# The rows between FFN forward and backward, stored by chunk of tokens instead of by feature group, with the order of the steps made anew

## The chip, the cores and the metric

The kernel runs on one core of a Trainium2 chip. The time is device microseconds of one execution, and the figure compared is the median of several. A core has a matrix engine (PE, whose weight loads the profile lists apart as PEld), three engines for elementwise work (VectorE or DVE, ScalarE or ACT, GpSimd or POOL), and SyncE (SP), which here only issues DMA transfers. Each engine works through its own list of instructions in order. A transfer is issued from the list of SP, ACT or POOL and lands some microseconds later; those of one list are issued one behind the other, and an issue that has to wait holds up all behind it.

## The reference

A block with a residual, and all of its gradients, in bf16:

```python
x = A_u                                   # 2048 tokens x 512 features
xn = layernorm(x)
s = conv_S4(xn, A, B, C, dt) + xn * Dskip # per feature a convolution of 2048 taps
g = silu(silu(xn @ w1) @ w2)              # w1 512x1792, w2 1792x512
out = x + s * g
# outputs: out, and the gradients for A_u, A_re, A_im, B_re, B_im,
#          C_re, C_im, log_dt, Dskip, w1, w2, from grad_out
```

The taps are `K = Re(sum over n of C P dB)` with `P = exp(dt A l)`, n of 128 states. The reference does the convolution by an FFT, the kernel by matrix products with DFT tables.

## The kernel before

The kernel is written as some forty generators, each a stream of steps: one step issues one block of matmuls, one eviction of PSUM, one elementwise instruction or one transfer. `PLAN` is seven strings, and every letter of them runs the next step of one stream; the order in the string is so the order on every engine. `SLOTS` gives the buffer that each tile takes. `WAYS` says for each stream which engine does its n-th PSUM eviction: A is ACT (line 116), D is DVE (line 117). Streams that the text speaks of:

- `F` (`gen_ffn_fwd`): for each of 8 chunks of 256 tokens, h = xn w1 in 7 pairs of feature groups (ps_h, L769), evicted to the tile `hT`, silu on ACT (L777), the product with w2 (ps_o, L786). The rows h, before silu, are stored to `Hd` in DRAM from POOL's list (`k.st`, L779), 8 feature groups and then 6.
- `X`, `C`: the forward convolution (ps_s L406, pt_f L420, ps_i L451 and L464, with evictions to `dA`, `dB`, `KE`). `R`: the taps (ps_k, L657, evicted to `ds`). `Kb` is a piece of the taps, read back.
- `D`, `B`: the same transforms for the gradient. `a`: loads h back from `Hd` into `dhT` (L1142, SP), `A`: multiplies with the gradient that comes through w2 (ps_da, L1174; L1177 on DVE) and stores the product to `DHd`. `x`: its product with w1 (ps_dx, L1198), evicted to `pd_s` or, for the last four, added on DVE (L1203).
- `Y`, `V`, `T`, `S`, `Z`: the gradients of the taps' parameters. In 32 halves of blocks `V` makes `Vb` (ps_v, L1026, evicted to `Vb`), `T` three products on DVE (L1043 twice, L1047), `S` a sum on PE (psS, L1063), `Z` the rest (L1087 to L1133).
- `h`, `t`, `w`: dW2. For each of 14 feature groups h is loaded back from `Hd` as `h_in` (L1217, SP), turned on PE and passed through silu (`a_tok`, L1228), and multiplied (ps_w, L1237), with an eviction to `o`. `g`, `v`: dW1, from `DHd`, by transposing loads `dh_tok` (L1252, SP) and ps_w (L1266) with evictions to `o` of 128x256.
- `i`, `k`, `m`: LayerNorm backward (L1307 on).

`Hd` is a tile of [14, 128, 2048]: feature group, feature, token. A store of a chunk therefore writes, for each feature and group, a run of 256 tokens or 512 bytes. The load of `dhT` reads the same runs. The load of `h_in` reads one feature group with all tokens, in runs of 4096 bytes. `DHd` lies in the same way.

Of the kernel before, what the change touches and what calls it, by code (L numbers as in the profile page):

```python
# [13 lines left out]
BF16 = mybir.dt.bfloat16  # L14
# [4 lines left out]
P = 128  # L19
# [27 lines left out]


SLOTS = dict(x.split("=") for x in """
fp.XT=01010101;pf.pf=012010210210210210201201201201210201201201201201201021021021012012012010210210210120120120120120210  # L50
210210210212010120120120120201202102102102102102102102102102102012012012102102102102101021012021021201021021012012120120
2102102012021021021021021;fp.hT=0101010101010101;fp.ob=0101010;dft.w8=21031230123102302103213032013201;pc.pc=01010101010
100010101010101010101010101010101010101010101010101010101101010101010101010101010101010101010101010101010101010101010101
010101010101010101010101010101010101001011010101010101010101010101010101011010101010101010101110101010101010010101010101
010101010101010;tbl.tv=01011010001010100101001011101010;tbl.ts=01010101010111011101010111010010;tbl.W=010101101011010110
10;dft.t4=010100101010;gate.S=01;gate.g=10672345;da.doT=01010101;da.dhT8=20120120;dftb.w8b=1010;da.dhT6=10101010;go.go_s
=01010101;go.go_r=010101;go.go_g=01010101;go.go_x=01201201;da.pd_s=010101010101;sb.YT=0120120120120120;sb.Eb=10101010;sb
.Gb=01010101;sb.Vb=0101010101010101;sb.Tp=0101010101010101;sb.Sa=1010;fw.h_in=01201201201201;fw.a_tok=10101010101010;fw.
o11=01201201201201;sb.g_acc=0101;fw.dh_tok=0120120;fw.o10=1010101;lw.pd_l=012301;lw.Gt=01230123;lw.m=010101;lw.o1=123012
30  # L60
""".replace("\n", "").split(";") if x)

WAYS = """J=DADAADAA;
F=DADAAAAAAAADDADAAAAAAAADAAAAAAAAAAAAAAAAAAADADDAAAAAAAAADAADDAADADDADAAA;
# [5 lines left out]
D=AAAADDAAAAAAAAADAAAAADAAAADAADAAAADAAADA;  # L72
d=DDAADDAA;
B=AAAAAAAAAADAAADAAAAAAAAAAAAAAAAAAAAAAAAAAAAADAAAAAAADAAD;
x=AAAAAAADAADD;
V=DAADAAAAADAAAAAADDAAAAAAAAAAAAAAAAAAAAAAAAAAAAAAAAAAAAAAAAAAAAAA;
Y=AAADDAAA;
w=ADAADAAAAAAAAA;
v=DAAAAAAAAAAAADAAAAAAAAAAAAAA"""


class Placed:
# [672 lines left out]
def gen_ffn_fwd(k):  # L755
    nc, fp = k.nc, k.fp
    D, FT, DK, T = k.D, k.FT, k.DK, k.T
    for c in range(T // 2):
        cs = slice(256 * c, 256 * c + 256)
        XTv = k.XT.pop(c)[:].rearrange("p (t k) n -> p t k n", k=DK)  # L760
        aT = fp.tile([P, FT, 256], BF16, name="aT", tag="aT", bufs=1)
        for f in range(FT // 2):
            if f in (0, 4):
                hT = fp.tile([P, 8, 256], BF16, name="hT", tag="hT", bufs=2)
            ps = k.pf.tile([P, 2, 256], F32, name="ps_h", tag="pf")
            for j in range(2):
                ft = 2 * f + j
                for dk in range(DK):
                    nc.tensor.matmul(out=ps[:, j], lhsT=k.W1[:, dk, ft * P:ft * P + P], rhs=XTv[:, :, dk, :],  # L769
                                     start=(dk == 0), stop=(dk == DK - 1))  # L770
            yield
            i = 2 * (f % 4)
            k.ev(hT[:, i:i + 2, :], ps[:])
            yield
            if f in (3, 6):
                f0, n = (0, 8) if f == 3 else (8, 6)
                nc.scalar.activation(out=aT[:, f0:f0 + n], in_=hT[:, 0:n], func=ACT.Silu)  # L777
# [558 lines left out]
def kernel(ctx, tc, A_u, A_A_re, A_A_im, A_B_re, A_B_im, A_C_re, A_C_im, A_log_dt, A_Dskip, B_x, B_w1, B_w2, grad_out,  # L1336
           out_0, out_1, out_2, out_3, out_4, out_5, out_6, out_7, out_8, out_9, out_10, out_11):
    nc = tc.nc
    k = KCtx()
    k.nc, k.tc = nc, tc  # L1340
    k.outs = [out_0, out_1, out_2, out_3, out_4, out_5, out_6, out_7, out_8, out_9, out_10, out_11]
    L, D, F = A_u.shape[1], A_u.shape[2], B_w1.shape[1]
    assert (L, D, F) == (2048, 512, 1792)
    k.L, k.D, k.F, k.T, k.DK, k.FT = L, D, F, 16, D // P, F // P
# [94 lines left out]
    sb = pool("sb", side="right", es=es_b)  # L1439
# [5 lines left out]
    fw = pool("fw")  # L1445
# [5 lines left out]
    lw = pool("lw", side="right")  # L1451
# [30 lines left out]
```

## Time and profile before

| | |
|---|---|
| runs | 575.15, 575.63, 578.03 us, median 575.63 |
| profiled execution | 573.44 us, span 571.7 |
| PE busy | 526.4 us (92%), weight loads 395.3 (69%) |
| DVE busy | 520.0 us (91%) |
| ACT busy | 446.6 us (78%) |
| POOL busy | 75.7 us (13%) |
| DMA moved | 144.49 MB, mean 253 GB/s |

The span is the part of the execution from the first to the last instruction in the profile. The busy times overlap, so that no sum of them is a time: an engine's share says how much room its list has, and the waits say which of the lists is late. Of a wait for several things the profile names the last to come, and where the named engine had long been done, a transfer is the likely one.

### The profile page before, as it was taken

The page shows a single profiled execution, that of the slowest core. Times are in us where ns is not written, and L with a number is a line of the kernel's source. Part 1 is how long each engine was busy: PE and PEld are TensorE (multiplying, and loading weights), DVE is VectorE, ACT ScalarE, POOL GpSimd, SP SyncE. Part 2 cuts the span into 40 slices and gives each one's busy share as a digit, 9 for nine tenths or more (in the row PEclk, how much of TensorE's full clock was granted, in tenths as well). Part 3 has the DMA queues.
Part 4 walks back from the last instruction along what each step waited for, and adds up shares of the span by engine and source line. Part 5 has one row for each costly group of instructions (what it writes and reads, how often), then busy time and mean ns, then how long its engine had stood idle before and what let it go on. Part 6 is the DMA issues. An engine that isn't in the chain of part 4 may idle for free.

```text
span 571.7 us, 14504 instructions
## 1 busy us (share of the span) xinstructions
PE 526.4 (92%) x5983; PEld 395.3 (69%) x6008; DVE 520.0 (91%) x817; ACT 446.6 (78%) x561; POOL 75.7 (13%) x164
## 2 busy tenths in 40 slices
PE   2499997999989989999999999999899999999994
PEld 1365876687768765876686766787578797786763
DVE  8999998999899959999999798979889999983994
ACT  6989998999989749998998776754476876754552
POOL 4251101010101020000000000000000030332122
PEclk9879999999999999999999999999999999999998
DMA  9988998998998988787978998898999989999693
GB/s 238 321 313 221 291 227 245 341 211 264 326 230 243 345 275 314 240 265 210 345 227 265 284 286 279 241 236 180 282 215 243 208 238 222 231 237 241 171 240 120
DMA packets 156643, 144.49 MB, mean 253 GB/s; under 512 B 83488, under 2 KB 132896, under 8 KB 153504
## 3 DMA queue, kind: packets, MB, share of 16 engines
q1 hardware_dynamic: 146816, 120.74, 79.2%
q0 software_dynamic: 6640, 19.67, 10.1%
q10 hardware_dynamic: 3120, 3.15, 1.7%
q8 instruction: 47, 0.77, 0.5%
q14 instruction: 20, 0.16, 0.1%
HBM read 62.78 MB, written 59.25 MB: 213 GB/s over the span
## 4 chain that ended last, share of the span: by engine, by line
PE 48%; DVE 17%; ACT 14%; issue 9%; DMA 8%; SPq 2%; POOL 1%; POOLq 0%; ACTq 0%; DVEq 0%
PE ps_dx L1198 7%; PE ps_da L1174 7%; PE ps_w L1237 5%; PE ps_w L1266 4%; PE ps_o L786 3%; PE ps_i L451 3%; PE ps_h L769 3%; ACT dA L116 3%; PE ps_i L464 3%; ACT mag_all L518 3%; PE pt_t L138 2%; PE ps_s L406 2%; DMA Ed<-ds 2%; ACT dB L116 2%; DMA dh_tok<-DHd 2%
## 5 line engine op out<-in xcount | busy, mean ns | idle before, releaser
L116 ACT CAST dA<-ps_s 128x1024 bf16<-128x1024 f32 x82 | 82.2, 1035 | 7.3 <-PE ps_s L406 5.1
L769 PE MATMUL ps_h<-XT,W 128*128 128x256 bf16 x448 | 59.5, 286 | 9.3 <-ACT hT L116 8.4
L116 ACT CAST Vb<-ps_v 128x672 bf16<-128x672 f32 x59 | 42.2, 733 | 27.7 <-PE ps_v L1026 17.9
L769 PEld LDWEIGHTS <-W 128*128 128x128 bf16 x448 | 44.4, 102 | 18.0 <-issue 9.8
L1174 PE MATMUL ps_da<-doT,W 128*128 128x256 bf16 x448 | 56.2, 273 | 0.0
L1266 PE MATMUL ps_w<-dh_tok,xn 128*128 128x256 bf16 x448 | 52.5, 273 | 0.7 <-DMA dh_tok<-DHd 0.4
L786 PE MATMUL ps_o<-W,aT 128*128 128x512 bf16 x213 | 50.3, 385 | 2.2 <-ACT aT L777 1.4
L1198 PE MATMUL ps_dx<-W,dhT 128*128 128x512 bf16 x224 | 50.9, 379 | 0.0
L1237 PE MATMUL ps_w<-YD,a_tok 128*128 128x512 bf16 x210 | 49.1, 379 | 1.3 <-ACT o L116 0.7
L116 ACT CAST dB<-ps_i 128x1024 bf16<-128x1024 f32 x42 | 41.6, 1029 | 8.1 <-PE ps_i L451 8.0
L1266 PEld LDWEIGHTS <-xn 128*128 128x128 bf16 x448 | 43.0, 98 | 6.6 <-issue 1.0
L1174 PEld LDWEIGHTS <-W 128*128 128x128 bf16 x448 | 41.6, 98 | 7.1 <-issue 0.8
L1177 DVE TENSOR_TENSOR dhT<-ps_da,dhT 128x512 bf16<-128x512 f32 x56 | 37.8, 686 | 5.5 <-PE ps_da L1174 3.9
L786 PEld LDWEIGHTS <-aT 128*128 128x128 bf16 x224 | 21.4, 99 | 27.0 <-issue 2.5
L1198 PEld LDWEIGHTS <-dhT 128*128 128x128 bf16 x224 | 21.1, 98 | 24.8 <-issue 1.6
L1237 PEld LDWEIGHTS <-a_tok 128*128 128x128 bf16 x224 | 21.6, 98 | 24.1 <-issue 0.8
L1228 ACT ACTIVATE a_tok<-pt_t 128x1024 bf16<-128x1024 bf16 x28 | 28.7, 1038 | 7.0 <-PE pt_t L138 6.9
L406 PEld LDWEIGHTS <-TF 128*128 128x128 bf16 x384 | 25.3, 101 | 8.3 <-issue 6.0
L584 ACT ACTIVATE sn<-V 128x1920 bf16<-128x1920 int16 x16 | 29.3, 1840 | 1.8 <-DVE V L580 1.7
L477 DVE TENSOR_TENSOR cm<-sp_in,dA 128x2048 bf16<-128x2048 bf16 x24 | 29.3, 1221 | 0.6
L479 DVE TENSOR_TENSOR sp_in<-sp_in,dA 128x2048 bf16<-128x2048 bf16 x24 | 29.3, 1222 | 0.6
L451 PE MATMUL ps_i<-I,sp_in 64*128 64x128 bf16 x768 | 27.2, 217 | 2.6 <-ACT KE L116 1.4
(243 smaller groups left out, 1230.6 us busy)
## 6 DMA issues: line engine op xcount, KB each, us to landing
Yd<-YD SPq DMA_DIRECT2D x8, 1024.0 KB, 5.6
sp_in<-Ud SPq DMA_DIRECT2D x8, 1024.0 KB, 8.3
h_in<-Hd SPq DMA_DIRECT2D x14, 512.0 KB, 5.6
Ed<-ds SPq DMA_DIRECT2D x8, 672.0 KB, 7.4
Eb<-Ed SPq DMA_DIRECT2D x8, 672.0 KB, 5.7
Hd<-hT POOLq DMA_DIRECT2D x8, 512.0 KB, 6.7
Ud<-dA SPq DMA_DIRECT2D x8, 512.0 KB, 7.3
KXd<-dA SPq DMA_DIRECT2D x4, 1024.0 KB, 6.4
```

Source lines behind the costliest of these rows:

```text
L116: return self.nc.scalar.copy(out=out, in_=in_)
L406: nc.tensor.matmul(out=ps[:, j], lhsT=k.TF[:, 8 * h + j, c, :], rhs=U(8 * h + j), start=True, stop=True)
L451: nc.tensor.matmul(out=ps[:, z, g], lhsT=Y[zs, c, g0 + g, :], rhs=k.I2[zs, c].rearrange("p c m -> p (c m)"), start=(c == 0), stop=(c == 1))
L477: TT(out=t2[:], in0=b[:, :, gs], in1=a[:, 1:2, gs].to_broadcast([P, 2, n, P]), op=ALU.mult)
L479: TT(out=b[:, :, gs], in0=b[:, :, gs], in1=a[:, 0:1, gs].to_broadcast([P, 2, n, P]), op=ALU.mult)
L769: nc.tensor.matmul(out=ps[:, j], lhsT=k.W1[:, dk, ft * P:ft * P + P], rhs=XTv[:, :, dk, :], start=(dk == 0), stop=(dk == DK - 1))
L786: nc.tensor.matmul(out=ps[:], lhsT=aT[:, ft, t * P:t * P + P], rhs=k.W2[:, ft, :], start=(ft == 0), stop=(ft == FT - 1))
L1174: nc.tensor.matmul(out=ps[:, j], lhsT=k.W2[:, ft, dk * P:dk * P + P], rhs=dTv[:, :, dk, :], start=(dk == 0), stop=(dk == DK - 1))
L1177: nc.vector.tensor_tensor(out=dh[:, i0:i0 + 2, :], in0=ps[:], in1=dh[:, i0:i0 + 2, :], op=ALU.mult)
L1198: nc.tensor.matmul(out=ps[:], lhsT=dhs[ft // 8][:, ft % 8, t * P:t * P + P], rhs=k.W1[:, :, ft * P:ft * P + P], start=(ft == 0), stop=(ft ...
L1237: nc.tensor.matmul(out=ps[:], lhsT=at[:, t, :], rhs=k.do[:, t, :], start=(t == 0), stop=(t == k.T - 1))
L1266: nc.tensor.matmul(out=ps[:], lhsT=k.xn[:, t, dk * P:dk * P + P], rhs=dh[:, t].rearrange("p j n -> p (j n)"), start=(t == 0), stop=(t == k ...
```

## The change

`Hd` becomes a tile of [8, 128, 14, 256]: chunk, feature, feature group, token in the chunk. The store writes a run of 4096 bytes for each feature (8 groups) or of 3072 (6 groups), and the load of `dhT` reads these. The load of `h_in` reads for each feature eight runs of 512 bytes, one of each chunk. What arrives in SBUF is the same. `DHd` is as it was.

```diff
@@ gen_ffn_fwd
-                k.st(k.Hd[f0:f0 + n, :, cs].rearrange("f p n -> p f n"), hT[:, 0:n])
+                k.st(k.Hd[c][:, f0:f0 + n, :], hT[:, 0:n])
@@ gen_da_loads
-            k.nc.sync.dma_start(dh[:, 0:n], k.Hd[f0:f0 + n, :, 256 * c:256 * c + 256].rearrange("f p n -> p f n"))
+            k.nc.sync.dma_start(dh[:, 0:n], k.Hd[c][:, f0:f0 + n, :])
@@ gen_dw2_loads
-        k.nc.sync.dma_start(h[:].rearrange("p t n -> p (t n)"), k.Hd[ft])
+        k.nc.sync.dma_start(h[:].rearrange("p (c u) n -> p c (u n)", u=2), k.Hd[:, :, ft, :].rearrange("c p n -> p c n"))
@@ pools
-    k.Hd = dr.tile([k.FT, P, L], BF16, name="Hd")
+    k.Hd = dr.tile([8, P, k.FT, 256], BF16, name="Hd")
@@ PLAN (the first line of the first string)
-22123515255p676p41674560J777577673J77077776757p71737607775p71777F87776FF3F6F7F867706168F644F760F663666786F487373636667F3F
+2311223p55556672641376p706176J3776747717pJ3576750F6776776761F637F78778707F706675p736636776770F7F65F7446466F86773F7663678
...
@@ WAYS
-F=DADAAAAAAAADDADAAAAAAAADAAAAAAAAAAAAAAAAAAAADADDAAAAAAAAADADAADDAADADDADAAA;
+F=DADAAAAAADADADAAAAAAAAADAAAAAAADAAAAAAAAAAAAADDAAAAAAAAADADDADADDADADDADAAA;
-R=DAAAAAAAAAAAAAAAAAADAADDDADADAAAAAAAADAAAAAAAAAA;
-C=DDDAAAAAAAAAAAAAAAAADDAAAAAAAADAAAAAADADDAADADAAADDDDDADAAAAAAAA;
+R=DAAAAAAAAAAADDAAAAADAAADDDDADAAAAAAAADDAAADDAAAA;
+C=DADAAAAAAAAAAAAAAAAADDAAAAADAAADAAAAAAADAAAAADDAADADAADDDDDADAAAAAAAA;
-D=AAAADDAAAAAAAAADAAAAADAAAAADAADAAADAAADAADA;
-d=DDAADDAA;
-B=AAAAAAAAAADAAADAAAAAAAAAAAAAAAAAAAAAAAAAAAAAADAAAAAAAADAAD;
-x=AAAAAAADAADD;
-V=DAADAAAAADAAAAAADDAAAAAAAAAAAAAAAAAAAAAAAAAAAAAAAAAAAAAAAAAAAAAAA;
-Y=AAADDAAA;
+D=AAAADDAAAAAAAAADAAADAAAAAAAADAAAAAAAAAAA;
+d=DDAAADAD;
+B=AAAAAAAAAADAAADAAAAAAAAAADADAAAAAADAAAADDAAAAAAAAAAAADADA;
+x=ADADDADDADAA;
+V=ADDAAADAAADAAAAADAAAAAADAADAAADAAAADAADADDAADADAAAAAAAAAAAAAAAAA;
+Y=DAAAAAAA;
-v=DAAAAAAAAAAAAADAAAAAAAAAAAAA
+v=AADDDADAADADAADAAAAAAAAAAAAAA
```

The tables are new throughout, and no step is added or left out. Evictions on DVE go from 90 to 110, those on ACT down by as many. Three places show what the tables do.

ACT in the head of the program, one piece of the difference. `mag_all` are magnitudes of the powers, `hT` the first rows of the FFN.

```order
 L513 ACT_TABLE_LOAD
 L513 ACTIVATE dt<-ldt 128x512
-L518 ACTIVATE mag_all<-lamr 128x8x64 x27
-L116 CAST hT<-ps_h 128x512
-L518 ACTIVATE mag_all<-lamr 128x8x64 x3
+L518 ACTIVATE mag_all<-lamr 128x8x64 x21
+L116 CAST hT<-ps_h 128x512
+L518 ACTIVATE mag_all<-lamr 128x8x64 x9
 L287 ACT_TABLE_LOAD
 L287 ACTIVATE warm<-onesf 128x1
```

The first eviction of `hT` moves forward by six steps of `mag_all`; the sum of these ahead of the table load stays 30.

DVE behind the last L1203, among the products of `T`, before:

```order
L1047 TENSOR_TENSOR Tp<-Tp,Tq 128x21x64
L117 CAST o_7164<-ps_w_7165 128x256
L1043 TENSOR_TENSOR Tp<-Vb,Eb 128x16x21x4
L117 COPY YT<-pt_y 128x1024
L1043 TENSOR_TENSOR Tq<-Vb,Eb 128x16x21x4
L1047 TENSOR_TENSOR Tp<-Tp,Tq 128x21x64
L1043 TENSOR_TENSOR Tp<-Vb,Eb 128x16x21x4
L1043 TENSOR_TENSOR Tq<-Vb,Eb 128x16x21x4
```

and the corresponding place now:

```order
L117 CAST Vb<-ps_v 128x672
L1043 TENSOR_TENSOR Tp<-Vb,Eb 128x16x21x4
L1043 TENSOR_TENSOR Tq<-Vb,Eb 128x16x21x4
L117 CAST o_7243<-ps_w_7358 128x256
L1047 TENSOR_TENSOR Tp<-Tp,Tq 128x21x64
L1043 TENSOR_TENSOR Tp<-Vb,Eb 128x16x21x4
L1043 TENSOR_TENSOR Tq<-Vb,Eb 128x16x21x4
L1047 TENSOR_TENSOR Tp<-Tp,Tq 128x21x64
L1043 TENSOR_TENSOR Tp<-Vb,Eb 128x16x21x4
L117 CAST Vb<-ps_v 128x672
```

Evictions of `Vb` and `o` that ACT did stand among DVE's products now, and the copy of `YT` has gone to ACT. In all DVE has behind the last L1203 9 evictions of `Vb` (2 before), 7 of `o` of 128x256 (2 before) and no `YT` (2 before); the rest of its list there is the same.

SP at the first loads of `dh_tok`, before (`Yn` and `Eb` belong to `Y`):

```order
L1217 DMA h_in<-Hd 128x2048
L1005 DMA Eb<-Ed 128x2688
L987 DMA Yn<-Yd 128x1024
L1252 DMA_TRANSPOSE dh_tok<-DHd 128x16x128 x2
L987 DMA Yn<-Yd 128x1024
L1217 DMA h_in<-Hd 128x2048
L1000 DMA_TRANSPOSE YT<-Yd 128x8x128 x2
L1217 DMA h_in<-Hd 128x2048
```

and now:

```order
L1005 DMA Eb<-Ed 128x2688
L1217 DMA h_in<-Hd 128x8x256
L987 DMA Yn<-Yd 128x1024
L1252 DMA_TRANSPOSE dh_tok<-DHd 128x16x128
L1217 DMA h_in<-Hd 128x8x256
L987 DMA Yn<-Yd 128x1024
L1252 DMA_TRANSPOSE dh_tok<-DHd 128x16x128
L1000 DMA_TRANSPOSE YT<-Yd 128x8x128 x2
```

The two halves of a `dh_tok` pair, which followed each other, have one load of `h_in` between them.

More of the change, by code (lines that the diff above doesn't have):

```diff
@@ new lines @@
+78FF8FF8F776F7F6F485F78/XJJFPFXFFXFXPXXFFXQXFFFPPFPJFFFFPFPFFJFFPFFUX9FQFPFQXXFRXXUFXRQFFXFQQQPQXJQFPQQFQPXRFPRXFRRRXFRF
+XFFPFQFFRQQQXXRFFQXUXFQFRRFRQFQQXJXPRFQRFPUXRPRPRRFFFRQRFFRRPFXQJRRJQXPPRRRXRRQFRXFRQFQCRFQXQFFQFRQXPQFXFFPRXRXRXFPCPRRR
+CQCPRXCRCCCFCQRUFFQRCRQCQQCCFCXFPQFXRQCQFCFCCFQPCQQCFRCRPXFRPRXRRFXFRRCCFQCQFXXCQCXRQFRPFCFQCFCCRRFRCFPRQXRCJRFQFFQCXRFR
+QRQFCCFCRPPCRXRCRPXJPPRRCCXFXFXQRFXCXPQFXFCXQXFQQQPFQCRFCXFFCFCQCRRCFUCQCQRPRFFFFQRFCCCFFCFRCFCFRCRJQCCRCCRRPRCPCXQCXFCC
+RQXXXCJPXRCQPQQQFFCQRCXPCRRRXQFCQCCFRRRCFRQCCFFXXRRFCFRCPRXPQRXFXXPFFRCCFRRFURFXCFFQXRCXFQRCCFCQCJCFQQRFCCCRRFQQQRFCQCCR
@@ new lines @@
+CRCRRRRCCFRRCCCRCRRCRRQRURCRCRCRCCC/JFCGCFCCGFGCFCGGCCCFFFFGCFCGCCGGFCCFCCFGCCGFGFCCCFFGCFGFCHCCFCGGFGGGGWCCHGCFGHFMCCFG
+CCCCCFCWGFCCCCHCCCWCGWWCWCCCWHDDGWWHWWHHCCCCWWLWDDWGWDWDWDDLWWWWMWWCDDDDLMWLLWDMWDMDDDD/addDDDdAEsWDasDdBDAAAoBoAABaAAoE
+ADABDADBABaBADDBAAADBABDosDABBAAAlBDABABOEDABBaoABADDBBOsoDxBBDBoBBBBAxxBBdABBOAlBoBOBOoxsOoDaOxDBAlxBBOBBBdoDADBBExoODx
+aDBDoxBOxDBsBBAlOAoBBBABoABxoDOdDBBBBdBBABAODBaADBoAADBAADBABAEBBBBsAAdAADDBBAAABOOABaDDoAoBOABBABODOOADlDoBsAxOxDAdoDox
+sDOABDAEoBDBBAOxxDAlAxDBBOoOABBxAOBDAABoaADBoBOAOBDABDdBAOABBODBxBBBoBDaDBDDxADxoBBxOBsxDBAOAAExOADBOoBsBABBoDAAdxBBDBBB
@@ L53 @@
[L53 to L57, printed above, removed]
@@ L58 @@
-.Gb=01010101;sb.Vb=0101010101010101;sb.Tp=0101010101010101;sb.Sa=1010;fw.h_in=01201201201201;fw.a_tok=10101010101010;fw.
-o11=01201201201201;sb.g_acc=0101;fw.dh_tok=0120120;fw.o10=1010101;lw.pd_l=012301;lw.Gt=01230123;lw.m=010101;lw.o1=123012
-30
+fp.XT=01010101;pf.pf=012012012012010212102102121221201201201201201201202102102102102102102101201201201021021021021021201
+201201201202121021201021021212102120120101010120120120120201201201201021021021021021021021020102102012120121010210210210
+1021012012012012121201210;fp.hT=0101010101010101;dft.w8=21031230123103103210320103120132;pc.pc=0101011010101101010101010
@@ new lines @@
+100101010101010101010010101010101010101010101010101010101010101010101101010101010101010101010101010101010110101010101010
+101011010101010101010101010101010101010101010101010101010101101010110101010101010010101010010111010101010101010100101010
+1;fp.ob=0101010;tbl.tv=01010110001010100101110101010101;tbl.ts=01011101010111010010101011010010;tbl.W=010101101011010110
+10;dft.t4=010100101010;gate.S=01;gate.g=10672345;da.doT=01010101;da.dhT8=01201201;dftb.w8b=1010;da.dhT6=10101010;go.go_s
+=01010101;go.go_r=010101;go.go_g=01010101;go.go_x=01201201;da.pd_s=101010101010;sb.YT=2012012012012012;sb.Eb=01010101;sb
@@ L61 @@
+.Gb=01010101;sb.Vb=0101010101010101;sb.Tp=0101010101010101;sb.Sa=0101;fw.h_in=01201201201201;fw.a_tok=10101010101010;fw.
+o11=01201201201201;sb.g_acc=0101;fw.dh_tok=0120120;fw.o10=1010101;lw.pd_l=012301;lw.Gt=10231023;lw.m=010101;lw.o1=120312
+03
 """.replace("\n", "").split(";") if x)
 WAYS = """J=DADAADAA;
-F=DADAAAAAAAADDADAAAAAAAADAAAAAAAAAAAAAAAAAAADADDAAAAAAAAADAADDAADADDADAAA;
+F=DADAAAAAADADADAAAAAAAAADAAAAAAADAAAAAAAAAAAAADDAAAAAAAAADADDADADADDADAAA;
 X=AAAAAAAAAAAAAAAAAAAAAAAAAAAAAADA;
@@ L78 @@
+d=DDAAADAD;
+B=AAAAAAAAAADAAADAAAAAAAAADADAAAAAADAAAADDAAAAAAAAAAAADADA;
+x=ADADDADDADAA;
+V=ADDAAADAAADAAAAADAAAAAADAAADAAAADAAADAADDAADADAAAAAAAAAAAAAAAAAA;
+Y=DAAAAAAA;
 w=ADAADAAAAAAAAA;
-v=DAAAAAAAAAAAADAAAAAAAAAAAAAA"""
+v=AADDDADAADADADAAAAAAAAAAAAAA"""
 class Placed:
```

32 lines of the change are left out of this document (8 added, 24 removed).

## The prediction

> **What bounds the kernel now.** I read the windows first, cut where the work changes: head to 40 us, forward convolution with the first FFN matmuls to 200, the rest of that to 245, the backward convolution with the FFN's gradients to 408.4, the kernel's gradients with dW2 and dW1 to 510.2, the end of these to 528.5, LayerNorm backward behind.
>
> ```profile
> 0.00:40.00 40.00, 20.39 (x120) 13.47 (x122) 37.22 (x102) 33.42 (x51) 17.48 (x67) 0.87 0.99 289
> 40.00:200.00 160.00, 151.63 (x1910) 115.06 (x1917) 155.15 (x203) 151.56 (x180) 15.58 (x21) 1.00 0.90 268
> 200.00:245.00 45.00, 41.28 (x547) 31.73 (x548) 36.73 (x46) 35.63 (x40) 4.93 (x8) 0.96 0.83 278
> 245.00:408.40 163.40, 161.85 (x1894) 117.95 (x1891) 150.15 (x203) 123.67 (x130) 6.48 (x12) 1.00 0.89 255
> 408.40:510.20 101.80, 99.42 (x1094) 78.65 (x1101) 98.17 (x157) 73.90 (x117) 17.00 (x31) 1.00 1.07 231
> 510.20:528.50 18.30, 18.20 (x168) 13.37 (x168) 7.76 (x24) 7.75 (x13) 5.53 (x10) 1.00 1.11 249
> 528.50:564.00 35.50, 33.58 (x267) 25.10 (x268) 34.81 (x88) 20.64 (x36) 8.20 (x14) 1.00 0.79 206
> ```
>
> The columns are the window, its length, then busy us of PE, PE's weight loads, DVE, ACT and POOL, the granted clock, the DMA share and GB/s. To 245 PE, DVE and ACT are all loaded and no one engine bounds. From 245 to 408.4 PE does (161.85 of 163.4), and DVE has 13.2 us free. In the fifth window PE has 2.4 us free, DVE 3.6, ACT 27.9: DVE and PE run in lockstep there. In the last, DVE has 0.7 us free. Which of the two sets the pace of the fifth, the groups on DVE in it show:
>
> ```profile
> L1047 DVE TENSOR_TENSOR Tp<-Tp,Tq 128x1344 bf16<-128x1344 bf16 x27 | 23.1, 855 | 0.6
> L1043 DVE TENSOR_TENSOR Tp<-Vb,Eb 128x1344 bf16<-128x1344 bf16 x27 | 23.0, 853 | 2.5 <-ACT Vb L116 2.4
> L1043 DVE TENSOR_TENSOR Tq<-Vb,Eb 128x1344 bf16<-128x1344 bf16 x27 | 23.0, 852 | 0.0
> L117 DVE CAST Vb<-ps_v 128x672 bf16<-128x672 f32 x2 | 1.7, 854 | 0.0
> L117 DVE COPY YT<-pt_y 128x1024 bf16<-128x1024 bf16 x2 | 1.4, 688 | 0.3 <-PE pt_y L991 0.3
> L117 DVE CAST o<-ps_w 128x256 bf16<-128x256 f32 x1 | 0.4, 418 | 0.0
> ```
>
> Three products for each of 27 blocks fill DVE, and of its 3.6 us of idle time 2.4 are waits for a Vb that ACT evicts. The chain through these products runs from the last addition of ps_dx (L1203), which lets DVE go on to them alone, to psS on PE and the last gradients. Beginning and end, with two rows that give the step from start to start of one Vb and one o:
>
> ```profile
> 407.70 0.69 DVE L1203 SCALAR_TENSOR_TENSOR ds<-ps_dx,ds 128x512 bf16<-128x512 f32 x1 [0.66 <-PE ps_dx L1198]
> ...
> 414.02 0.85 DVE L117 CAST Vb<-ps_v 128x672 bf16<-128x672 f32 x1
> 414.78 0.85 DVE L1047 TENSOR_TENSOR Tp<-Tp,Tq 128x1344 bf16<-128x1344 bf16 x1
> ...
> 520.91 0.42 DVE L117 CAST o<-ps_w 128x256 bf16<-128x256 f32 x1 [1.96 <-PE ps_w L1266]
> 521.25 0.27 DVE L1131 TENSOR_TENSOR g_acc<-pd,dt 1x128 bf16<-1x128 f32 x1
> 528.53 0.69 DVE L1307 SCALAR_TENSOR_TENSOR pd_l<-pd_l,ds 128x512 bf16<-128x512 bf16 x1 [7.01 <-ACT a_tok L1228]
> ```
>
> **The change, part by part: DVE behind the last L1203.** Up to there PE's list has the same length, and behind it DVE's lists differ only in evictions: Vb 2 before and 9 now, o of 128x256 2 and 7, YT 2 and 0. A Vb costs 414.78 - 414.02 = 0.76, an o 521.25 - 520.91 = 0.34, a YT its 0.69 less the overlap of 0.09 that Vb shows (0.85 against 0.76), 0.60. So DVE gets 7 x 0.76 + 5 x 0.34 - 2 x 0.60 = 5.32 + 1.70 - 1.20 = +5.8 us. ACT is relieved of as many, but its 27.9 free us show that it was not the bound. At most the work fills all of DVE's 3.6 us of idle time and 2.2 us show; at least nothing of it and 5.8 do. I take half of the 2.4 us of Vb waits as saved (a Vb made on DVE itself is no longer waited for from ACT, but some 43 of 52 stay there), 1.2, so **+4.6**. What is late next is Tp, hence psS, and the lists on PE behind it.
>
> In one sentence beside this, a rule that speaks for the upper end: the Trainium skill, page "Perfetto Trace Analysis", section "Identifying the Most-Contended Engine", calls matmul busy time a poor measure for the tensor engine, takes weight-load busy time instead, and names the engine of highest occupancy as the one to look at. By it the fifth window is DVE's (98.17 of 101.8, 96%, against 78.65, 77%, for weight loads), all 5.8 us would show, and the median come out at 581.4 instead of 580.2; the row of 2.4 us of waits for ACT is why I don't take all.
>
> **DVE and ACT ahead of it.** Of all evictions DVE does 90 before and 110 now: the ten net ones above, and ten ahead of the last L1203. There dA goes from 14 to 9, ds of ps_k from 6 to 12, dB of ps_i from 6 to 9 and pd_s from 3 to 6; of seven other kinds five have one more and two one less.
>
> ```profile
> L117 DVE CAST dA<-ps_s 128x1024 bf16<-128x1024 f32 x14 | 16.8, 1220 | 6.5 <-PE ps_s L406 6.0 <-PE ps_s L434 0.5
> L117 DVE CAST dB<-ps_i 128x1024 bf16<-128x1024 f32 x6 | 7.3, 1222 | 0.6 <-PE ps_i L451 0.4
> L117 DVE CAST ds<-ps_k 128x336 bf16<-128x336 f32 x6 | 3.0, 498 | 0.0
> L117 DVE CAST pd_s<-ps_dx 128x512 bf16<-128x512 f32 x3 | 2.1, 684 | 0.0
> ```
>
> 6 x 0.50 + 3 x 1.22 + 3 x 0.68 - 5 x 1.22 = 3.0 + 3.7 + 2.0 - 6.1 = +2.6 us, and the net three others at most 3 x 1.22 = 3.7 more. The dB and pd_s, and most of the rest, fall in the PE-bound window to 408.4, whose 13.2 free us on DVE cover even 6.3; if that cover were gone it would cost between 2.6 and 6.3. Term 0.
>
> **Waits in the convolution.** The steps are mixed anew. The single waits on PE that a new mix can reach are these:
>
> ```profile
> 94.23 1.05 PE L406 MATMUL ps_s<-Kb,TF 128*128 128x128 bf16 x16 [2.17 <-DMA Kb<-KE]
> 168.57 0.62 PE L451 MATMUL ps_i<-I,sp_in 64*128 64x128 bf16 x16 [1.39 <-ACT KE L116]
> 212.09 1.86 PE L406 MATMUL ps_s<-Kb,TF 128*128 128x128 bf16 x16 [2.30 <-issue]
> 213.75 1.86 PE L769 MATMUL ps_h<-XT,W 128*128 128x256 bf16 x8
> ```
>
> Ahead of the first, eight more ps_h matmuls now stand between ps_f and Kb, 1.9 us by the row of such a block at 213.75, so it may go from 2.17 to 0.3; the place of 212.09 is the same as before. Against it stands what three more ps_k on DVE delay there, 3 x 0.50 = 1.5. Term 0, from -1.9 to +1.5.
>
> **Head.** ACT does 30 magnitude steps, now 21 ahead of the first hT and 9 behind, where it was 27 and 3. The sum is the same, so the second hT and the silu behind it stay where they are.
>
> ```profile
> PE pt_t L138 <- DVE xn L390: 10.0, 1, 10.0
> PE ps_h L769 <- ACT hT L116: 8.4, 2, 4.3
> 28.65 1.91 ACT L777 ACTIVATE aT<-hT 128x2048 bf16<-128x2048 bf16 x1
> ```
>
> The loads of x stand earlier on SP, so the first wait of 10.0 us may shrink, but what is won waits again for that silu at 28.65. Term 0; at most +1 if the W1 parts, now behind x, come late.
>
> **The store, the two loads and the queues.** Rows of DMA issues (KB each, median us to landing) and one of the queues:
>
> ```profile
> q0 software_dynamic: 6640, 19.67, 10.1%
> h_in<-Hd SPq DMA_DIRECT2D x14, 512.0 KB, 5.6
> Hd<-hT POOLq DMA_DIRECT2D x8, 512.0 KB, 6.7
> dhT<-Hd SPq DMA_DIRECT2D x8, 512.0 KB, 6.5
> dh_tok<-DHd SPq DMA_TRANSPOSE x14, 7.2
> 483.31 11.22 DMA dh_tok<-DHd
> PE ps_w L1266 <- DMA dh_tok<-DHd: 0.4, 1, 0.4
> ```
>
> The store goes over POOL's queue, q0, whose packets are 19.67 MB / 6640 = 3.0 KB already though the runs are 512 B; no engine's waits name it. Term 0. The dhT load gets longer runs, by the nearest row (h_in, 4 KB runs, the same bytes) 5.6 for 6.5 us; it runs ahead of its use and saves nothing. The h_in load gets 512 B runs, by the dhT row 6.5 for 5.6, 0.9 each, 14 times. Three h_in buffers cover the tile itself. But the DMA share in the fifth window is 1.07, and the transposes of dh_tok, queued behind h_in on SP, arrive just as PE wants them: 11.2 us on the chain, PE late by 0.4, once. Two h_in ahead of one pair: +1.8; the other way, the 0.4 goes: -0.4. I take 0, since 6.5 us are still less than the 7.2 of a transpose and the pairs now stand with one h_in between their halves.
>
> The Trainium skill, page "DMA: Bandwidth & Descriptors", section "Specifications", puts the least transfer for line rate at 512 B. By it the h_in load in runs of just that length loses nothing and the sum is the same; by the dhT row it lands 0.9 us later each time. Where the two differ, the row decides, and rival 3 stands on it.
>
> **Tail.** POOL's gout and g_acc stores now stand without an out store ahead of them, which frees half a microsecond at best; DVE's first L1307 at 528.53 had waited 7.01 us, put down to an a_tok long done, so for stores that land. The list of DVE from L1307 is the same. Term 0, from -0.5.
>
> **Sum.** The profiled execution took 573.44 us, its span 571.7, so 1.7 lie around it; the median of the runs, 575.63, stands 2.2 above it. 573.4 + 4.6 = 578.0 for an execution like the profiled one, and **580.2** as a median. From 575.63 half a per cent, 2.9 us, is about what a measurement tells from no change: 572.75 to 578.5.
>
> **Rivals.** (1) Faster: the new mix takes the three waits of 2.17, 2.30 and 1.39 (5.9) from the convolution and the last L1203 comes that much earlier, while DVE swallows the evictions down to 2.2. Then 573.4 + 2.2 - 5.9 + 2.2 = 571.9. It decides once L1203 is 5.1 earlier with 2.2, or 7.5 with 4.6. For it: one place grew by eight matmuls. Against: the place of 212.09 is the same, and up to 200 us three engines are over 94% busy. (2) Same: DVE's 3.6 us of idle time absorb all they can, since more Vb there mean fewer waits for ACT: 573.4 + 2.2 + 2.2 = 577.8. It holds if the Vb waits are gone. (3) Slower by the loads: h_in in 512 B runs makes each of seven dh_tok pairs late by 0.9, and PE, with 2.4 free, waits each time: 4.6 + 6.3 less the 0.4 that PE waits now, 573.4 + 10.5 + 2.2 = 586.1. For it the DMA share of 1.07; against it PE waited for dh_tok once in all. (4) The longer runs of the store and dhT do nothing at all: that is in the forecast, as both terms are 0.
>
> **How the numbers follow.** The forecast 0.50 (its own range 578.6 to 582.5), rival 1 0.13, rival 2 0.27, rival 3 0.10. Faster 0.13, same 0.27, slower 0.50 + 0.10 = 0.60. The range goes from 574.0, rival 1's waits with 4.6 in the fifth window (574.3), to 586.0, rival 3.
>
> **What would show it.** Of after: L1203's last row within 2 us of 407.7; DVE's Vb row in the stretch behind it with 9 and the wait of Tp for Vb on ACT below 2.4; that stretch to the last Tp longer by some 4.6 than 101.8; the h_in row near 6.5 and dhT near 5.6; PE's wait for dh_tok below 1.8. If L1203 moves by more than 3 us either way, the new mix of the convolution, not the evictions, made the time, and the prediction is wrong even if its number is near.

## The result: 1.4% slower, and the profile after

The changed kernel takes 583.94 us as a median (581.91 to 584.63), the kernel before 575.39. The ratio is 1.0138, with a 95% interval of 1.0093 to 1.0183. The profiled execution of the changed kernel took 584.63 us at a span of 582.8. So the two profiles stand 11.2 us apart where the medians stand 8.5: the profiled execution of before was the shortest of its runs, that of after the longest.

The span can be cut at five events that both kernels have: the first ps_da on PE, the last row of L1203 on DVE (its accumulator read), the start of the last L1047, the first L1307, and the end of the span. Windows of before with these cuts (window, its length, busy us of PE, PEld, DVE, ACT, POOL, granted clock, DMA share, GB/s):

```profile
0.00:248.90 248.90, 216.72 (x2614) 162.59 (x2626) 233.01 (x357) 224.50 (x272) 37.99 (x96) 0.97 0.89 271
248.90:408.30 159.40, 158.33 (x1851) 115.52 (x1849) 146.15 (x193) 119.68 (x126) 6.48 (x12) 1.00 0.90 258
408.30:509.40 101.10, 98.72 (x1089) 78.03 (x1096) 97.47 (x158) 73.42 (x117) 17.00 (x31) 1.00 1.07 231
509.40:528.50 19.10, 19.00 (x175) 14.09 (x175) 8.56 (x24) 8.32 (x14) 5.53 (x10) 1.00 1.11 248
528.50:571.70 43.20, 33.58 (x267) 25.10 (x268) 34.82 (x88) 20.64 (x36) 8.74 (x15) 0.95 0.68 179
```

The same of after:

```profile
0.00:246.70 246.70, 216.10 (x2604) 160.58 (x2617) 234.24 (x361) 223.41 (x267) 35.40 (x96) 0.98 0.87 274
246.70:409.60 162.90, 159.62 (x1855) 115.91 (x1853) 150.13 (x199) 118.15 (x121) 6.48 (x12) 1.00 0.85 254
409.60:518.70 109.10, 100.50 (x1094) 78.67 (x1104) 102.80 (x167) 68.48 (x106) 16.53 (x30) 1.00 1.01 218
518.70:537.20 18.50, 18.25 (x166) 13.44 (x166) 8.84 (x25) 8.02 (x13) 6.86 (x12) 1.00 0.90 231
537.20:582.80 45.60, 34.06 (x274) 25.39 (x274) 35.18 (x88) 21.32 (x36) 7.99 (x14) 0.94 0.58 164
```

| stretch | before | after | difference |
|---|---|---|---|
| to the first ps_da | 248.9 | 246.7 | -2.2 |
| from there to the last L1203 | 159.4 | 162.9 | +3.5 |
| to the last L1047, the stretch of products | 101.1 | 109.1 | +8.0 |
| to the first L1307 | 19.1 | 18.5 | -0.6 |
| to the end of the span | 43.2 | 45.6 | +2.4 |

In the stretch of products DVE is busy 5.3 us longer (102.80 against 97.47), and its idle time grows from 3.6 to 6.3. What it waits for there, the groups of after show (busy, mean ns, idle before and releaser at the end of a row):

```profile
L1043 DVE TENSOR_TENSOR Tp<-Vb,Eb 128x1344 bf16<-128x1344 bf16 x27 | 23.0, 852 | 0.2
L117 DVE CAST Vb<-ps_v 128x672 bf16<-128x672 f32 x9 | 7.7, 851 | 2.5 <-PE ps_v L1026 2.5
L117 DVE CAST o<-ps_w 128x256 bf16<-128x256 f32 x5 | 2.1, 415 | 0.0
L1103 DVE TENSOR_TENSOR gout<-g_t,dt 128x512 bf16<-128x512 f32 x3 | 2.1, 686 | 2.8 <-DMA out_dram<-gout 2.8
```

The 2.4 us in which Tp waited for a Vb from ACT are down to 0.2. But DVE waits 2.5 us for PE ahead of the Vb that it evicts itself. And there is a wait that before doesn't have at all: L1103 writes the gradients `gout` into their only buffer and stands 2.8 us until POOL's stores of the group before have landed. The group of before, then timelines of DVE and POOL after:

```profile
L1103 DVE TENSOR_TENSOR gout<-g_t,dt 128x512 bf16<-128x512 f32 x3 | 2.1, 685 | 0.0
```

```profile
506.16 0.69 DVE L1103 TENSOR_TENSOR gout<-g_t,dt 128x512 bf16<-128x512 f32 x1 [2.83 <-DMA out_dram<-gout]
537.19 0.69 DVE L1307 SCALAR_TENSOR_TENSOR pd_l<-pd_l,ds 128x512 bf16<-128x512 bf16 x1 [6.86 <-DMA out_dram<-gout]
```

```profile
497.33 3.19 POOL L1125 DMA_DIRECT2D out_dram<-gout  x6 [6.72 <-ACT gout L1122]
```

The six stores are issued from 497.33 to 500.52, and L1103 of the next group is ready only 3 us behind the last of these. The same place in before:

```profile
489.05 3.18 POOL L1125 DMA_DIRECT2D out_dram<-gout  x6 [2.81 <-ACT gout L1122]
497.27 0.69 DVE L1103 TENSOR_TENSOR gout<-g_t,dt 128x512 bf16<-128x512 f32 x1
```

There L1103 comes 5.0 us behind the last of the stores and doesn't wait. The profile after names the stores for L1307 too, for which the one before named a_tok.

PE's waits ahead of the stretch of products, from 246.7 to 409.6, where the second term of the table arose (us in total, times, longest):

```profile
PE ps_v L1026 <- ACT YT L116: 1.0, 1, 1.0
PE ps_v L1026 <- ACT Gf L971: 0.6, 1, 0.6
PE ps_v L1026 <- ACT Vb L116: 0.5, 1, 0.5
PE G L968 <- DVE Vb L117: 0.5, 1, 0.5
```

PE is idle for 162.9 - 159.6 = 3.3 us there, and was for 1.1 before; the other 1.3 us of the +3.5 are busy time of PE, with 1855 matmuls recorded in the window where there were 1851. Of the loads and stores that changed their runs, those of 512 KB land within 0.7 us of before (us to landing, and last the row of POOL's queue):

```profile
h_in<-Hd SPq DMA_DIRECT2D x14, 512.0 KB, 5.7
Hd<-hT POOLq DMA_DIRECT2D x8, 512.0 KB, 7.4
dhT<-Hd SPq DMA_DIRECT2D x8, 512.0 KB, 5.9
q0 software_dynamic: 6384, 19.67, 9.3%
```

### The profile page after: what moved, and what is told of

Its sections match the earlier page's. It is cut to its first block, busy times and chain, and to the rows that moved or that the text cites. A ratio compares the mean times of both kernels' runs of the same rounds, so it can differ in the third digit from the quotient of the medians.

```text
span 582.8 us, 14505 instructions
## 1 busy us (share of the span) xinstructions
PE 528.5 (91%) x5983; PEld 394.0 (68%) x6008; DVE 531.2 (91%) x837; ACT 439.4 (75%) x541; POOL 73.3 (13%) x164
## 2 busy tenths in 40 slices
DMA packets 156643, 144.49 MB, mean 248 GB/s; under 512 B 83488, under 2 KB 132896, under 8 KB 153504
## 3 DMA queue, kind: packets, MB, share of 16 engines
q0 software_dynamic: 6384, 19.67, 9.3%
## 5 line engine op out<-in xcount | busy, mean ns | idle before, releaser
L116 ACT CAST dA<-ps_s 128x1024 bf16<-128x1024 f32 x87 | 86.5, 1030 | 3.9 <-PE ps_s L434 1.9
L116 ACT CAST Vb<-ps_v 128x672 bf16<-128x672 f32 x51 | 36.1, 732 | 25.2 <-PE ps_v L1026 20.1
L116 ACT CAST dB<-ps_i 128x1024 bf16<-128x1024 f32 x39 | 38.6, 1019 | 11.1 <-PE ps_i L451 11.0
L1266 PEld LDWEIGHTS <-xn 128*128 128x128 bf16 x448 | 43.2, 98 | 5.1 <-issue 0.2
L1026 PE MATMUL ps_v<-Gb,YT 128*128 128x168 bf16 x256 | 27.1, 236 | 5.9 <-ACT Vb L116 3.2
L477 DVE TENSOR_TENSOR cm<-sp_in,dA 128x2048 bf16<-128x2048 bf16 x24 | 29.3, 1221 | 1.7 <-DMA sp_in<-Ud 0.8
L479 DVE TENSOR_TENSOR sp_in<-sp_in,dA 128x2048 bf16<-128x2048 bf16 x24 | 29.3, 1222 | 0.6
```

Of the source, the lines that this page charges most:

```text
L116: return self.nc.scalar.copy(out=out, in_=in_)
L477: TT(out=t2[:], in0=b[:, :, gs], in1=a[:, 1:2, gs].to_broadcast([P, 2, n, P]), op=ALU.mult)
L479: TT(out=b[:, :, gs], in0=b[:, :, gs], in1=a[:, 0:1, gs].to_broadcast([P, 2, n, P]), op=ALU.mult)
L1266: nc.tensor.matmul(out=ps[:], lhsT=k.xn[:, t, dk * P:dk * P + P], rhs=dh[:, t].rearrange("p j n -> p (j n)"), start=(t == 0), stop=(t == k ...
```

## Experiments: layout or order

Runs of one set share the runs of before. The first set takes the change apart into the layout of `Hd` and the tables. The layout alone:

```diff
 (after.py, with PLAN, SLOTS and WAYS of before)
```

> The new layout of Hd with the old tables of order, buffers and evictions. The theory (the evictions moved to DVE behind the last L1203, and a wait that the new order makes there, cost the time; the layout costs nothing) expects a time within 1.5 us of before, an h_in load at 5.6 to 6.5 us, and the stretch from the last L1203 to the last L1047 at about 101.8 us. The rival that the 512-byte runs of h_in cost it expects 5 us or more above before, with PE waiting for dh_tok or h_in.

Measured: ratio 1.0067 (1.0035 to 1.0099), 579.7 us beside 574.52. That lies between the two expectations, and it is a loss where the theory had none. The stretch of products is 100.9 us, h_in lands in 5.5 us, and PE waits 0.4 us for a dh_tok, as in before. The profiled execution took 577.11 us, so it shows 3.6 us of span beside before's profile. The largest loss, 3.4 us, lies between the first ps_da and the last L1203. The timeline of PE, and the windows there:

```profile
399.53 0.62 PE L991 MATMUL pt_y<-ident,Yn 128*128 128x128 bf16 x8 [2.06 <-DMA Yn<-Yd]
399.99 0.45 PE L1026 MATMUL ps_v<-Gb,YT 128*128 128x168 bf16 x4
400.28 7.89 PE L1198 MATMUL ps_dx<-W,dhT 128*128 128x512 bf16 x28
```

```profile
396.00:400.00 4.00, 1.95 (x24) 1.57 (x23) 3.67 (x7) 0.72 (x1) 0.00 (x0) 1.00 1.01 327
400.00:404.00 4.00, 4.00 (x17) 1.69 (x15) 0.86 (x1) 1.63 (x2) 0.00 (x0) 0.57 0.92 263
404.00:408.00 4.00, 4.00 (x20) 1.76 (x18) 2.33 (x4) 0.00 (x0) 0.00 (x0) 1.00 1.18 195
```

PE waits 2.06 us for a transfer of Yn (0.53 before), and behind that wait the granted clock falls to 0.57 for some 4 us: the 28 matmuls of ps_dx take 7.89 us where they took 6.21 before. The wait and the clock give 1.5 + 1.7 = 3.2 us. Why Yn, which isn't part of the layout, comes later is not shown; two runs below with the old layout and the old order up to this place (pad7 and the second buffer in before) wait 1.76 and 1.20 us for it, so the wait differs between executions and is no mark of the layout.

The rest of this profile is 2.8 us gained up to the first ps_da, 1.5 lost ahead of L1307, whose wait is 8.52 us here, and 1.8 behind L1307. The last is a cost that goes with the layout. The last store that POOL issues, in before and in after:

```profile
564.31 0.54 POOL L1331 DMA_DIRECT2D out_dram<-o  x1 [1.58 <-DVE o L1329]
573.70 0.54 POOL L1331 DMA_DIRECT2D out_dram<-o  x1 [1.04 <-DVE o L1329]
```

From the start of that store the span of before goes on for 7.4 us, that of after for 9.1. In the six kernels where the store and the dhT load keep their short runs it is 7.3 to 7.4, in the eight with the new layout 9.1 to 9.2, whatever the tables. No engine is busy behind that store and the transfers are over some 2 us from its start, so where the 1.8 us go is not shown.

The tables alone:

```diff
 (before.py, with PLAN, SLOTS and WAYS of after)
```

> The old layout of Hd with the new tables. The theory expects the whole loss, 6 to 10 us above before, with a stretch from the last L1203 to the last L1047 of 109 to 111 us and the wait of L1103 for the gout store in it (2 to 3 us). If the layout made the loss, the time is within 2 us of before.

Measured: 1.0139 (1.0092 to 1.0187), the whole loss. The stretch of products is 110.2 us, and L1103 waits 4.16 us for the stores. By the times the layout adds nothing that can be told with the new tables and 0.7% with the old ones, so the two are not terms of a sum. The longer end comes with the layout under either set of tables; a difference of 1.8 us lies within the intervals here.

## Experiments: the engines of the evictions

All evictions of the changed kernel back on their old engines, its order kept:

```diff
-F=DADAAAAAADADADAAAA...   (all rows of WAYS)
+F=DADAAAAAAAADDADAAAA...
```

> The changed kernel with all evictions back on the engines that they had before; its order and buffers stay new. The theory expects 5 to 8 us less than the changed kernel, so 0 to 3 us above before: what is left is the wait of L1103 for the gout store. If the new order alone made the loss (the rival), it stays 6 us or more above before.

Measured: 1.0362 (1.032 to 1.0405), slower by far than the changed kernel. The expectation failed. DVE has the few Vb of before in the stretch of products, and it takes 113.4 us; the groups of DVE there:

```profile
L1043 DVE TENSOR_TENSOR Tp<-Vb,Eb 128x1344 bf16<-128x1344 bf16 x27 | 23.0, 853 | 6.3 <-ACT Vb L116 6.3
L1103 DVE TENSOR_TENSOR gout<-g_t,dt 128x512 bf16<-128x512 f32 x3 | 2.1, 687 | 3.0 <-ACT Vb L116 3.0
L117 DVE COPY YT<-pt_y 128x1024 bf16<-128x1024 bf16 x2 | 1.4, 692 | 4.8 <-PE pt_y L991 4.8
```

The order was made for the engines that the new table names. With others the products wait 6.3 us for Vb where they wait 0.2, and DVE 4.8 us for PE ahead of the YT that it copies again. The reverse, the kernel before with the new engines:

```diff
-F=DADAAAAAAAADDADAAAA...   (all rows of WAYS)
+F=DADAAAAAADADADAAAA...
```

> The kernel before with the new choice of engines for the evictions alone. The theory expects 4 to 6 us above before, most of it behind the last L1203 (that stretch 105 to 108 us for 101.8). If evictions hide in idle time of DVE, it stays within 2.5 us of before.

Measured: 1.0308 (1.0262 to 1.0354), more than three times what was expected, with 115.0 us for the stretch and 5.8 us lost ahead of it. In the stretch PE waits up to 4.09 us for DVE, and the granted clock over it is 0.96, so part of its length is the clock. So neither run prices the moved evictions. They show that order and engines can't be changed apart here.

## Experiments: DVE's work and the wait for the stores

The price of work on DVE in the stretch of products, with nothing moved: the kernel before writes Tq twice in seven places.

```diff
+                if c == 1 and r == 0 and i in (4, 6, 8, 9, 10, 12, 13):
+                    (the same tensor_tensor into Tq once more)
```

> The kernel before with seven of the products Tq written twice behind the last L1203: 7 x 0.77 = 5.4 us more work for DVE there, with nothing else moved. If DVE sets the pace of the stretch and only its idle time can absorb work, it grows by 2.2 to 5.4 us, and the time with it; the prediction's term for as much work was 4.6. If the loss of 8 us is that of any added DVE work, it grows by 8.

Measured: 1.0065 (1.0033 to 1.0097), 578.03 us beside 574.65. The window from its last L1203 to the last product:

```profile
407.70:513.80 106.10, 100.14 (x1095) 78.53 (x1101) 103.15 (x164) 74.29 (x117) 17.07 (x31) 1.00 1.00 227
```

DVE is busy 103.15 - 97.47 = 5.7 us longer and the stretch 106.1 - 101.1 = 5.0. In the stretch nine tenths of the work show; the idle time shrinks only from 3.6 to 3.0, so work that stands elsewhere in the list hardly fills it. In the time 3.4 us show (1.9 to 5.6 by the interval): L1307 comes 18.0 us behind the last product, where it came 19.1, and that gives a part back.

The kernel after once more, as the neighbour of the next runs:

> The changed kernel once more, beside the next three. 7 to 10 us above before, as first measured, and the stretch from the last L1203 to the last L1047 at 109 us or more.

Measured: 1.0137 (1.0106 to 1.0167), stretch 109.5 us.

A second buffer for gout in the changed kernel; the even groups write into a tile that also serves as `jk`, the scratch of L1308:

```diff
-    out = sb.tile([P, 6, P], BF16, name="gout", tag="gout")
+    out = sb.tile([P, 6, P], BF16, name="gout", tag="gout") if b % 2 else k.gout
@@
-    k.jk = fw.tile([P, D], BF16, name="jk")
+    k.gout = fw.tile([P, 6, P], BF16, name="gout_even")
+    k.jk = k.gout[:].rearrange("p a n -> p (a n)")[:, 0:D]
```

> The changed kernel with a second buffer for gout, so that L1103 need not wait until the stores of the group before have landed. If that wait is on the path, the stretch from the last L1203 to the last L1047 gets 2 to 3 us shorter than in the changed kernel (106 to 107 for 109.1) and the time 2 to 3 us less. If other waits take its place, the time stays within 1 us of the changed kernel.

Measured: 575.24 us, 1.0014 (0.9993 to 1.0035). The time is back at that of before, 7.3 us below the changed kernel against the 2 to 3 expected. The stretch of products is as expected:

```profile
406.60:512.70 106.10, 99.54 (x1088) 77.96 (x1096) 102.69 (x167) 68.08 (x104) 16.46 (x30) 1.00 1.04 221
```

106.1 us, 3.0 shorter than after, with the same work on DVE: this is the wait of L1103. The rest comes behind it. L1307 starts 12.7 us behind the last L1047 and not 18.5:

```profile
512.74 0.86 DVE L1047 TENSOR_TENSOR Tp<-Tp,Tq 128x1344 bf16<-128x1344 bf16 x1
...
525.41 0.69 DVE L1307 SCALAR_TENSOR_TENSOR pd_l<-pd_l,ds 128x512 bf16<-128x512 bf16 x1 [0.48 <-DMA pd_l<-Pd]
```

The edit had done two things, since another first user of the memory changed which bytes `pd_l` takes over. Two runs take them apart. One buffer for gout, in the pool of the dW streams, keeps L1103's wait and removes L1307's:

```diff
-    out = sb.tile([P, 6, P], BF16, name="gout", tag="gout")
+    out = k.fw.tile([P, 6, P], BF16, name="gout", tag="gout")
```

> The changed kernel with gout still in one buffer, but in the memory of the dW streams, so that pd_l of LayerNorm backward no longer takes over memory from which gout is stored. It tells the two waits apart that the second buffer took away: L1103's for the stores (here it stays, stretch at 109 us or more) and L1307's (here it goes: L1307 12 to 14 us behind the last L1047 instead of 18.5). If both are on the path, the time is 3 to 5 us below the changed kernel; if L1307's is not, within 1 us of it.

Measured: 578.32 us, 1.0071 (1.0044 to 1.0099), about 4 us below the changed kernel. Stretch 109.1 us with L1103's wait in it, and L1307 at 12.8 behind the last product:

```profile
504.24 0.69 DVE L1103 TENSOR_TENSOR gout<-g_t,dt 128x512 bf16<-128x512 f32 x1 [2.64 <-DMA out_dram<-gout]
529.55 0.69 DVE L1307 SCALAR_TENSOR_TENSOR pd_l<-pd_l,ds 128x512 bf16<-128x512 bf16 x1 [1.16 <-DMA pd_l<-Pd]
```

Two buffers the other way round, so that the last group's stores leave from the memory that L1308 overwrites:

```diff
+    out = sb.tile([P, 6, P], BF16, name="gout", tag="gout") if b % 2 == 0 else k.gout
```

> The changed kernel with two buffers for gout, the other way round: the last group's stores leave from the memory that jk (L1308) overwrites, so L1308 has to wait for them, as L1307 does in the changed kernel. L1103's wait goes alone. If it is on the path, the stretch is 106 us and the time 2.5 to 4 us below the changed kernel; if not, within 1 us of it.

Measured: 581.46 us, 1.0118 (1.0079 to 1.0157). The stretch is 106.2 us as expected, and L1308 waits 6.73:

```profile
532.91 0.69 DVE L1308 SCALAR_TENSOR_TENSOR gout_even<-pd_l,xn 128x512 bf16<-128x512 bf16 x1 [6.73 <-ACT o L116]
```

The trace shows the 3 us in the stretch. The time is 1.1 us below the changed kernel's in the run beside gout2, with intervals that overlap, so as a saving of time this wait by itself isn't shown; the one behind the products is, and both together are. A part is lost again at the stores: L1308 starts 9.8 us behind the first of the last group's stores (issued at 523.11), where after's L1307 starts 8.4 behind (528.81). Why these land later is not shown.

The engines of dW1's evictions as before, on top of the second buffer:

```diff
-v=AADDDADAADADADAAAAAAAAAAAAAA
+v=DAAAAAAAAAAAAADAAAAAAAAAAAAA
```

> The second gout buffer (as in the run that took the loss away), and the evictions of dW1's o on the engines that they had before, five fewer on DVE in the stretch of products: 5 x 0.34 = 1.7 us less there. If DVE's work passes through, the stretch is 104.5 us for 106.2 and the time 1 to 2 us below that run, at or below before; if the order does not fit these engines any more, it is longer.

Measured: 576.9 us, 1.0039 (1.0014 to 1.0064), and a stretch of 108.2 us in place of 104.5. The expected 1 to 2 us less did not come. This profile was the longest of its runs (580.57 us), and the clock was down at the head of its stretch:

```profile
410.00:414.00 4.00, 3.27 (x37) 2.99 (x35) 3.79 (x4) 2.60 (x4) 0.00 (x0) 0.76 1.10 305
414.00:418.00 4.00, 3.15 (x41) 2.95 (x40) 3.18 (x5) 2.32 (x4) 0.00 (x0) 0.81 1.00 259
```

The lowered clock alone is worth some 1.7 us there, an estimate from 4 x (0.24 + 0.19). So it isn't shown whether the order again doesn't fit other engines, or the clock made the stretch longer.

## Experiments: the runs of h_in, and a faster kernel

Only the h_in load in eight runs of 512 bytes, with the old order:

```diff
-    k.Hd = dr.tile([k.FT, P, L], BF16, name="Hd")
+    k.Hd = dr.tile([k.FT, P, 8, 272], BF16, name="Hd")
@@ (store and dhT load: [..., c, 0:256], runs of 512 bytes as before)
-        k.nc.sync.dma_start(h[:].rearrange("p t n -> p (t n)"), k.Hd[ft])
+        k.nc.sync.dma_start(h[:].rearrange("p (c u) n -> p c (u n)", u=2), k.Hd[ft][:, :, 0:256])
```

> The kernel before with its old order and Hd padded to 272 tokens for each chunk: store and dhT load keep their 512-byte runs, and only the h_in load changes, from runs of 4096 bytes to eight of 512. If the runs of h_in cost the 3.9 us of the layout alone, it is 3 to 5 us above before; if they cost nothing, within 1.5 us of before, and the layout's loss comes from the store and the dhT load.

Measured: 1.0022 (0.9992 to 1.0052), no difference that can be told, and its upper end leaves three quarters of the 0.7% open. This profile too shows the wait for Yn (1.93 us) and a clock of 0.63 behind it. The span goes on for 7.3 us from the last store, as in before, so the 1.8 us at the end go with the store or the dhT load and not with h_in's runs. What makes the rest of the layout's 0.7% stays open.

The second buffer in the kernel before:

> The kernel before with the second gout buffer alone. Nothing waits for the buffer in its stretch, which stays at 101 us; L1307, which waits 7 us for the stores in it, starts 5 us or more earlier, but PE has only some 2 us free behind the products and is the next bound: 1 to 3 us below before, faster than both kernels. If L1307's wait was not on the path, no change.

The edit is that of gout with `k.gout` for even groups. Measured: 571.98 us beside 574.83, ratio 0.9961 (0.9926 to 0.9995), faster than both kernels, if barely clear of before. The stretch stays at 100.9 us, L1307 starts 11.9 us behind it where it was 19.1, and PE has no idle time left: from 510 to 560 us it is busy throughout.

```profile
510.00:530.00 20.00, 20.00 (x186) 14.89 (x184) 14.08 (x41) 9.79 (x16) 6.43 (x12) 1.00 1.12 250
530.00:560.00 30.00, 30.00 (x242) 22.44 (x240) 27.97 (x69) 18.31 (x32) 7.32 (x13) 1.00 0.75 227
```

This run also corrects a reading of gout2. L1307's wait is nearly the same in both kernels (7.01 us before, 6.86 after), so it is no cause of the difference between them; taking it away makes either faster. With the second buffer in both, the new kernel is still 0.5% slower (1.0014 and 0.9961), some 3 us, with intervals that just touch.

## Why the prediction was right, and which steps were mis-sized

The time lies in the range (574.0 to 586.0), on the forecast side, and 3.7 us above the forecast; it lies above the likeliest case's own range, which ended at 582.5. The range reached up to 586.0 only for rival 3, late transposes of dh_tok, and none of them was late; so that the time fell inside it is in part luck. The mechanism forecast for the stretch of products held, but from profile to profile the difference is +11.2 us where +4.6 were forecast, and what the sum left out or put at nothing (+3.0 for L1103's wait, +3.5, +2.4) stands against gains of 2.2 and 0.6. Of the signs that were named, the last L1203 starts 1.3 us later (409.02), within 2 us, but as a sum of -2.2 and +3.5; DVE has its 9 Vb, and Tp's wait fell; the stretch is 8.0 us longer in place of some 4.6. By the steps:

- **The stretch of products, +4.6, measured +8.0.** The mechanism held: DVE's added evictions lengthen it. Two sizes were off. I took half of the 2.4 us of waits for Vb as saved. They did fall, to 0.2, but 2.5 us of waits of DVE for PE took their place, and pad7 shows that work passes through at 5.0 of 5.7. So in the stretch the work was worth 5.1 (106.2 in the run without the wait, 101.1 before), nearer to the upper bound of 5.8 than to 4.6. In the time pad7 cost 3.4 us, which tells neither from the other. The other 3.0 are the wait of L1103 for the gout stores, which no term had. The sentence that DVE's lists behind L1203 differ only in evictions was true and not enough: the place of L1103 against POOL's stores is set by the order as well, and I compared counts, not distances.
- **The rule on the most contended engine** (the Trainium skill, "Perfetto Trace Analysis", "Identifying the Most-Contended Engine"), which the prediction read as all of the added work showing, came nearer in the stretch than the half that I took: pad7's 5.0 of 5.7, and an idle time of 3.4 us with the second buffer where it was 3.6.
- **Waits in the convolution, 0 (from -1.9 to +1.5), measured -2.2.** The three quoted waits, 5.9 us, are gone from the profile, as rival 1 had it; what it wins back differs between executions (-2.2 in the first profile, -6.2 in the second of the same kernel). Rival 1 was partly there and was outweighed. One row was misread: the block of ps_h at 213.75 took 1.86 us because it ran behind the wait at 212.09, at a granted clock of 0.58 over 4 us; the same block at 208.75, with the clock at 1.00, takes 1.04. Eight more such matmuls fill 1.0 us, not 1.9.
- **DVE and ACT ahead of the products, 0, measured +3.5.** The 13.2 us of idle time on DVE were a cover for DVE alone. PE waits 2.6 us in four places for YT, Gf and Vb, which come from ACT and DVE, and 1.3 us more of PE's work lie on this side of the cut. The seven profiles with the new order and, up to this place, the new engines all have 162.9 or 163.0 us here, so this is no accident of one execution. An average of idle time over 160 us covered the work, but not its last places; which of the moved steps makes these waits, no run tells.
- **Store and loads, 0.** Right by the times with the new tables (1.0139 without the layout, 1.0138 with it) and for h_in's landing, 5.7 where the dhT row gave 6.5. dh_tok was not waited for, and rival 3 fell. Wrong for the layout with the old tables, 0.7%, and by the 1.8 us at the end of the span, for which the prediction had no row; what makes the rest of the 0.7%, the runs don't settle. On the DMA page's rule (the Trainium skill, "DMA: Bandwidth & Descriptors", "Specifications") the trace of h_in agrees: 5.7 for 512-byte runs, 5.6 for 4096. The 512 KB dhT load leans the other way, 6.5 and 5.9.
- **Head 0, measured +0.6** (the silu at 28.65 starts at 29.3), within its bound; **tail 0, measured -0.6** ahead of L1307 and +2.4 behind it, of which 1.8 are the longer end that goes with the layout.
- **The stores at the tail.** The prediction read L1307's 7.01 us as stores that land, against the profile's name for it. gout_fw shows that: with other memory the wait is 1.16, and for another transfer. What the prediction didn't ask was what this wait costs in both kernels: about 4 us in the changed one (gout_fw), 2.9 in before.
- **Rival 2**, 577.8 with all idle time filled, falls with pad7's stretch. Its condition, that the Vb waits go, came true (0.2 us), and the idle time stayed.

## What to carry to other kernels

Where a new order is judged by lists, compare for each buffer that leaves by a store the distance between the store's issue and the next write, not only the counts of instructions: a single-buffered output cost 3 us of the stretch here though its work was the same. Work added to the engine that sets the pace of a stretch showed nearly whole in that stretch (5.0 of 5.7 us), and the engine's idle time was no reserve, since it sat at hand-overs that the work didn't reach. An order and the engines that it was made for belong together; an experiment that swaps one of them measures the mismatch (+3% here) and not the part. Where one change removes a loss, try it in the kernel before as well: the second buffer made both faster, so not all that it won was the loss.

## What the runs showed of the hardware

A wait of PE can cost more than itself. In the run with the layout alone PE waited 2.06 us, and the granted clock was 0.57 over the next 4 us; with h_in's runs alone 1.93 us and 0.63. A matmul of ps_dx took up to 635 ns there and 379 otherwise. Waits at the same place of 1.76 (pad7), 1.20 (the second buffer in before) and 0.53 (before) left the clock at 1.00.

The length of the wait alone doesn't decide. At the ps_s block near 212 us, a wait of 2.30 us was followed by a clock of 0.58 over 4 us (before), and one of 2.82 by 1.00 (the layout alone):

```profile
212.09:216.09 4.00, 4.00 (x36) 3.48 (x37) 1.22 (x1) 2.96 (x3) 0.45 (x1) 0.58 1.03 346
210.87:214.87 4.00, 4.00 (x51) 3.67 (x52) 2.81 (x3) 3.35 (x3) 0.00 (x0) 1.00 1.05 398
```

What else decides, the traces don't show. The Trainium skill, "TensorE: Matmul & The Clock Gate", section "Why this matters for your kernels", asks for no idle gap over about 3 us. A wait of 3.64 us at that block (h_in's runs alone, clock 0.57) agrees; here shorter ones were enough in some executions and not in others.

The length of the runs in DRAM showed a little in the landing times. For h_in the rows of all runs give 5.5 to 6.2 us with 512-byte runs and 5.4 to 5.6 with 4096. For the dhT loads they give 6.3 to 6.9 with 512-byte runs and 5.9 to 6.2 with 4096 (512 KB), 4.8 to 5.9 and 4.1 to 5.0 with 3072 (384 KB). The packets hardly changed: POOL's queue moved its 19.67 MB in 6640 packets with stores of 512-byte runs and in 6384 with runs of 3 and 4 KB, and all queues together moved 156643 in both kernels.
